# A routed kernel: five visits get the split second product, and the third token tile another PSUM bank

## The chip, the cores and the metric

The kernel runs on one core of a Trainium2 chip. A time is device microseconds (us) of one execution. Beside the plain runs there is one execution that was recorded instruction by instruction; all rows below come from it. PE is TensorE, PEld its weight loads, DVE is VectorE, ACT is ScalarE, POOL is GpSimd and SP is SyncE, which here only issues transfers. A small q (SPq, POOLq) is the sequencer of an engine. [...]

## The reference, cut to what matters

Two stages. The first is a convolution over time with seven taps whose weights come from a softmax per position and head; the second is a mixture of experts with two levels of choice, 4 groups of 4 experts, one expert per token.

```
w = softmax(weight_gen, axis=-1)                      # 8 x 2880 positions, 8 heads, 7 taps
x = sum_k w[:, s, h, k] * x_pad[:, s + k, h, :]       # 23040 tokens of 192
g = argmax(x @ w_group);  e = argmax(x @ w_expert[g])
out = softmax(..)[g] * softmax(..)[e] * (relu(x @ w1[g, e]) @ w2[g, e])   # w1 192x1024, w2 1024x192
```

## The kernel before

**Front and visits.** The tokens are cut into fifteen groups of 1536. For each group the front makes the softmax, the convolution in two chunks of six columns (`conv`; a chunk is seven products and six additions on DVE, 128x1152 each), the scores (`logits`: six pieces, each of three transposes on PE and a copy by ACT, then 48 small matmuls and a last transpose), the ranking (`ranks`, on DVE) and twelve scatters of token rows by POOL (`scatter_row`) into a table sorted by expert. Behind some groups a table of visits is made (`table`, `listing`). A visit takes 128, 256 or 384 rows of one expert, loads its rows and weights through SP (`load`: part 0 rows `xb`, parts 1 and 2 the first weights, part 3 the second), transposes the rows on PE (`prep_x`), and does the two products (`gemm1`, `gemm2`). What comes out is scaled and written to its places by POOL (`send`, L962). `ROUNDS` says how many visits of which size stand behind which group. The last four rounds are: behind the twelfth group one visit of 384 and four of 256; behind the thirteenth (index 11 of `ROUNDS`) five of 256; behind the fourteenth (index 12) six of 256; behind the fifteenth and last (index 13) ten of 384, six of 256 and two of 128. Behind the fifteenth group POOL also writes sixteen blocks of padding rows (L559).

**Order of the work.** PE, ACT, DVE and SP run in the order in which the program emits their instructions. The emission is interleaved by a planner with clocks of its own (`clk`). A visit is a row of units: four of two slices of the inner width for 256 rows, eight of one slice for 384. In a unit the planner emits `gemm1` of the unit, then preparations for the next visit (at unit 0 `block(nxt)` and the copy `prep_d`, at unit 1 `prep_x(nxt, 0)`, and for a visit of 384 its third tile, `prep_x(nxt, 2)`, at unit `last // 2 + 1`, which is 2 while a visit of 256 runs and 4 while one of 384 does), then `gemm2` of the unit two before (`LAG`), then at most one weight split, then what waits in the queues `late`, `held` and `later` (DVE work, by `flush`), and at last `fill`, which takes steps of the front until DVE's planned clock is ahead of PE's by `AHEAD`.

**A step of the front.** `step()` resumes the front's generator until it next yields a cost. Beside the convolution, `routing` moves the scores by one piece per unit and only when the ranking of the group ahead is done. Behind the last group's convolution nothing is left but `settle`, which moves with a limit of 99; in `move` that limit lifts the one piece per unit:

```
if what == "time" and v > clk["dve"] or what == "unit" and v == state["unit"] and most < HURRY or ...:
    return
```

So the step that ends the last chunk of the last group (it sets `o.chunks` to 2) goes on and emits every remaining piece of `logits`, the 48 matmuls and the last transpose before it comes to the first cost, that of `ranks`.

**Whole and split second product.** `whole(n)` is true for visits of 128 and, below the round `WHOLE`, for the others. A whole visit keeps hidden values and second weights as float32 and does one matmul of 192 columns per slice and token tile (L945). A split visit rounds the hidden values (`hh`, L918), makes their remainder on DVE (`hl`, DVE at L840 into `pr`), casts the second weights on ACT (L832) and makes their remainder on DVE, in two halves of a visit (`split`, part 3), and does a matmul of 384 columns (L947) and one of 192 (L948) per slice and tile. The remainder's scaled add is one more DVE instruction per tile (L960). The weights of a split visit arrive in one buffer (`raw[2]`), so the next visit's part 3 is asked for when the second half is split. `hl` takes the three `pr` buffers of the convolution, so no convolution may come after the first split visit; `block` sees to that by taking all steps of the front.

**Banks.** `tpx` (pool `ps_x`, one bank) takes the transposed rows of two tiles, or of the third tile. ACT copies them out rounded (`xh`, L887) and DVE makes the remainder (`xl`, L840) from the same bank; until then the bank is not free. `tp` (pool `ps_t`, one bank) is used by the visits of 128, at L870 to L874, and by every other piece of `logits` (L387 to L399). The rows `xb` of a visit of 256 lie in a buffer that was that of the visit six before, and its part 0 waits until POOL's writes of that visit have landed, as they read their places from it.

Of the kernel before, what the change touches and what calls it, by code (L numbers as in the profile page):

```python
# [9 lines left out]
F32 = mybir.dt.float32  # L10
# [9 lines left out]
WIDTHS = (12,) * 15  # L20
# [3 lines left out]
HURRY = 12  # L24
SPACED = range(2, 15)
HALVES = (36.0, 42.0, 48.0, 54.0, 60.0, 66.0, 72.0, 78.0)
WHOLE = 12
SINGLE = tuple((k,) for k in range(7))
MIXED = ((0, 1), (2,), (3,), (4,), (5,), (6,))
TURNED = ((6, 5), (4,), (3,), (2,), (1,), (0,))  # L30
# [11 lines left out]
def conv_moe_kernel(ctx: ExitStack, tc: tile.TileContext, x, wgen, w_group, w_expert, w1, w2, out):  # L42
# [5 lines left out]
    P = 128  # L48
# [7 lines left out]
    SC = 6  # L56
# [13 lines left out]
    ENDS = [r[0] for r in ROUNDS]  # L70
# [27 lines left out]
    ps_x = pool("ps_x", 1, space=PSUM)  # L98
    ps_t = pool("ps_t", 1, space=PSUM)
# [12 lines left out]
    grp = {}  # L112
# [129 lines left out]
    def run(eng, cost, *deps):  # L242
        clk[eng] = max([clk[eng]] + [d + HOP for d in deps]) + cost
        return clk[eng]
# [484 lines left out]
    def step():  # L729
        c = next(fr, None)  # L730
        if c is None:
            return False
        if isinstance(c, Until):
            clk["dve"] = max(clk["dve"], c)
        elif c is not NEXT:
            run("dve", c + 0.06)
        if state["starve"] or not state["slots"] and c is NEXT:
            state["unit"] += 1
        return c
# [18 lines left out]
    def plain(n):  # L758
        return order[n][1] == 1
# [107 lines left out]
    def prep_x(b, t0):  # L867
        fill(b.o.tx)
        if b.plain:
            tp = ps_t.tile([P, 3, P], F32, name="tp")  # L870
# [5 lines left out]
            b.txl = 0.0  # L876
            return
        m = min(2, b.nt - t0)
        tp = ps_x.tile([P, 2, 2, P], F32, name="tpx")[:, :, 0:m]
        for t in range(m):  # L880
            nc.tensor.transpose(out=tp[:, 0, t, :], in_=b.x[:, t0 + t, 0:P], identity=ident)  # L881
            nc.tensor.transpose(out=tp[:, 1, t, :], in_=b.xd[:, t0 + t].rearrange("p a b -> p (a b)"), identity=ident)  # L882
# [94 lines left out]
    def whole(n):  # L977
        r, nb, q = order[n]
        return nb == 1 or n < nmain and r < WHOLE

# [8 lines left out]
    def blocks(n0, n1, paced):  # L989
# [44 lines left out]
        def block(i):  # L1034
            n = units[i][0]
            o = visits[n]
            b = Slot()
            b.th = {}
            b.plain, b.nt = plain(n), order[n][1]
            b.wide = b.nt == 3  # L1040
            b.nv = 1 if b.wide else 2
            b.n = b.nt * P
            b.o, b.h, b.x = o, {}, o.xb
            b.clears = n == nmain - 4
            if not b.plain:
                while state["open"]:
                    assert step() is not False
                state["slots"] = True
            if not o.whole:
                while step() is not False:  # L1050
                    pass
            return b

        lead = range(n0, min(n0 + 3, n1))
# [28 lines left out]
        for i in range(len(units) + LAG):  # L1083
# [25 lines left out]
            if i < len(units):  # L1109
# [7 lines left out]
                for job in list(jobs):  # L1117
                    m, part, h = job
# [60 lines left out]
```

## Time and profile before

| | |
|---|---|
| median of 3 runs | 1201.04 us (1196.92 to 1202.0) |
| the profiled execution | 1193.24 us, of it 1191.6 us span |
| mean granted clock of TensorE | 0.989 |
| busy share of the span | PE 95%, PEld 90%, DVE 81%, ACT 55%, POOL 48% |

Busy time of a matmul overlaps with the next one's, since matmuls are pipelined; so steps on PE are measured from start to start here, and not by adding durations. Times in the rows are from the span's start.

### The profile page before, as it was taken

What the parts mean: (1) busy time and instruction counts of PE and PEld (TensorE: products, weight loads), DVE (VectorE), ACT (ScalarE), POOL (GpSimd) and SP (SyncE); (2) the same over time, 40 slices, a digit from 0 to 9 for tenths busy, and PEclk for the clock granted to TensorE, in tenths of its full rate; (3) what the DMA queues carried; (4) which work ended last, traced back from release to release, by engine and by line L of the source; (5) the groups of instructions that cost most, each with busy time, mean ns of one, the idle gap of its engine ahead of it and who ended that gap; (6) DMA issues with size and microseconds to landing.
All of it is one profiled execution on the core that took longest, in us unless ns stands there. A gap on an engine that the chain in (4) does not pass through costs nothing.

```text
span 1191.6 us, 24474 instructions
## 1 busy us (share of the span) xinstructions
PE 1132.8 (95%) x8357; PEld 1073.7 (90%) x8357; DVE 959.7 (81%) x1646; ACT 651.2 (55%) x1235; POOL 569.1 (48%) x608
## 2 busy tenths in 40 slices
PE   5787899999999999999999999999999989999998
PEld 3444788999999999999999999999899989999997
DVE  8899898999998999899999999898535756666661
ACT  1331345565565655655655655655556766666572
POOL 6154183756273747575656555374664112222211
PEclk9997999999999999999999999999999999999999
DMA  5698799887888877888687878558688675555562
GB/s 172 212 308 224 264 303 308 267 266 249 255 253 261 282 221 239 274 253 264 211 298 228 281 223 293 186 160 257 203 271 256 217 196 159 160 161 159 164 200 76
DMA packets 82758, 275.08 MB, mean 231 GB/s; under 512 B 15063, under 2 KB 31734, under 8 KB 80832
## 3 DMA queue, kind: packets, MB, share of 16 engines
q1 hardware_dynamic: 62296, 229.76, 61.9%
q0 software_dynamic: 20208, 43.39, 11.5%
q8 instruction: 67, 1.10, 0.4%
q14 instruction: 67, 0.55, 0.2%
q10 hardware_dynamic: 120, 0.28, 0.1%
HBM read 225.83 MB, written 48.42 MB: 230 GB/s over the span
## 4 chain that ended last, share of the span: by engine, by line
PE 58%; issue 20%; DVE 7%; DMA 6%; POOL 5%; SPq 2%; ACT 1%; POOLq 1%; DVEq 0%; ACTq 0%
PE py L945 26%; PE ph L907 24%; POOL out L962 4%; DVE pr L294 3%; PE pl L375 2%; DMA raw<-w1lo 1%; PE tpx L882 1%; DMA out<-y,xb 1%; PE tpx L881 1%; DMA wt<-in_weight_gen 1%; DMA w1lo<-raw 1%; DMA xb<-rows 1%; PE ph L335 1%; PE tp L392 1%; POOLq L557 1%
## 5 line engine op out<-in xcount | busy, mean ns | idle before, releaser
L907 PE MATMUL ph<-xh,wa 128*128 128x256 f32 (+1 forms) x1992 | 465.5, 307 | 0.0
L962 POOL DMA_INDIRECT out<-y,xb x189 | 204.9, 1084 | 438.7 <-DVE y L960 193.8
L945 PE MATMUL py<-wc,hh 128*128 128x192 f32 x2160 | 399.9, 326 | 2.1 <-ACT y L954 2.1
L907 PE MATMUL ph<-xl,wa 128*128 128x256 f32 (+1 forms) x1328 | 360.2, 290 | 0.3 <-DVE xl L840 0.3
L945 PEld LDWEIGHTS py<-wc,hh 128*128 128x128 f32 x2160 | 346.4, 190 | 2.4 <-ACT y L954 2.3
L907 PEld LDWEIGHTS ph<-xh,wa 128*128 128x128 f32 x1992 | 337.5, 190 | 3.3 <-issue 1.8
L913 ACT ACTIVATE hh<-ph 128x512 f32<-128x512 f32 (+2 forms) x296 | 165.5, 559 | 262.0 <-PE ph L907 261.8
L294 DVE TENSOR_TENSOR pr<-xin,wt 128x1152 f32<-128x1152 f32 x186 | 248.9, 1350 | 5.5 <-PE py L335 3.5
L907 PEld LDWEIGHTS ph<-xl,wa 128*128 128x128 f32 x1328 | 251.9, 190 | 0.6 <-DVE xl L840 0.6
L503 POOL DMA_INDIRECT rows<-xrow,ix x156 | 227.4, 1457 | 49.4 <-POOL ix L502 35.8
L312 DVE TENSOR_TENSOR xrow<-xrow,pr 128x1152 f32<-128x1152 f32 x144 | 194.6, 1351 | 0.7
L840 DVE SCALAR_TENSOR_TENSOR pr<-ph,hh 128x384 fp32r<-128x384 f32 (+1 forms) x128 | 77.5, 606 | 99.8 <-ACT hh L918 98.6
L840 DVE TENSOR_TENSOR wa<-raw,wa 128x1024 fp32r<-128x1024 f32 x83 | 101.4, 1222 | 31.1 <-ACT wa L816 30.9
L947 PE MATMUL py<-wc,hh 128*128 128x384 f32 x352 | 110.6, 362 | 0.0
L918 ACT ACTIVATE hh<-ph 128x384 fp32r<-128x384 f32 (+1 forms) x128 | 68.4, 534 | 69.8 <-PE ph L907 69.8
L502 POOL COPY ix<-posi 128x1 int32<-128x1 int32 x156 | 70.0, 458 | 63.7 <-DMA rows<-xrow,ix 36.2
L816 ACT CAST wa<-raw 128x1024 fp32r<-128x1024 f32 x83 | 87.2, 1050 | 3.1 <-DMA raw<-in_moe_w 3.1
L948 PE MATMUL py<-wc,pr 128*128 128x192 f32 x352 | 88.0, 250 | 0.0
L825 ACT CAST wa<-raw 128x1024 fp32r<-128x1024 f32 x83 | 86.7, 1045 | 0.6 <-DMA raw<-w1lo 0.6
L954 ACT ACTIVATE y<-py,xb 128x192 f32<-128x192 f32 x179 | 67.1, 422 | 21.4 <-PE py L945 19.7
L840 DVE TENSOR_TENSOR xl<-tpx,xh 128x512 fp32r<-128x512 f32 (+1 forms) x94 | 61.5, 655 | 17.0 <-ACT xh L887 16.2
L948 PEld LDWEIGHTS py<-wc,pr 128*128 128x128 f32 x352 | 67.1, 191 | 0.0
(178 smaller groups left out, 1341.8 us busy)
## 6 DMA issues: line engine op xcount, KB each, us to landing
wc<-in_moe_w SPq DMA_DIRECT2D x73, 768.0 KB, 5.8
raw<-in_moe_w SPq DMA_DIRECT2D x83, 512.0 KB, 5.4
xin<-in_x SPq DMA_DIRECT2D x14, 1728.0 KB, 10.0
raw<-in_moe_w SPq DMA_DIRECT2D x91, 256.0 KB, 5.2
raw<-w1lo SPq DMA_DIRECT2D x83, 256.0 KB, 5.4
raw<-in_moe_w SPq DMA_DIRECT2D x22, 768.0 KB, 6.8
xb<-rows SPq DMA_DIRECT2D x72, 194.0 KB, 3.8
wa<-in_moe_w SPq DMA_DIRECT2D x24, 384.0 KB, 5.0
```

The lines of the kernel that those rows point to most:

```text
L294: nc.vector.tensor_tensor(out=dst, in0=o.xin[:, c0 + k:c0 + k + SC, :].rearrange("p s (h g) -> p s h g", g=HG), in1=w4[:, c0:c0 + SC, :, k ...
L312: nc.vector.tensor_tensor(out=acc, in0=acc, in1=prs[k - 2], op=ALU.add)
L503: written_once(nc.gpsimd.indirect_dma_start(out=rows[:, :], out_offset=bass.IndirectOffsetOnAxis(ap=ix, axis=0), in_=src, in_offset=None, ...
L816: nc.scalar.copy(out=o.wa[:, 0, :], in_=o.raw[0])
L825: nc.scalar.copy(out=o.wa[:, 2, :], in_=o.raw[1])
L840: f(*a, **k)
L907: nc.tensor.matmul(ph[:, v, :], lhsT=w[:, f0:f0 + P], rhs=rhs, start=i == 0, stop=i == len(terms) - 1)
L913: nc.scalar.activation(out=hh, in_=ph, func=AF.Relu)
L945: nc.tensor.matmul(b.acc[t], lhsT=hh[:, v, c], rhs=wc[0][:, f, :], start=f == 0 and not (b.wide and t == 1), stop=f == NFT - 1 and not (b. ...
L947: nc.tensor.matmul(b.py[t], lhsT=hh[:, v, c], rhs=wc[f // 4][:, f % 4].rearrange("p l d -> p (l d)"), start=f == 0, stop=False)
L948: nc.tensor.matmul(b.acc[t], lhsT=hl[:, v, c], rhs=wc[f // 4][:, f % 4, 0, :], start=False, stop=f == NFT - 1)
L962: ins = nc.gpsimd.indirect_dma_start(out=out[:, :], out_offset=bass.IndirectOffsetOnAxis(ap=b.x.bitcast(I32)[:, t, D + 1:D + 2], axis=0), ...
```

## The change

Three edits. `WHOLE` goes from 12 to 11, so the five visits of 256 behind the thirteenth group become split ones. The third tile of a visit of 384 (`t0` is 2) is transposed into `tp` instead of `tpx`; that concerns the ten visits behind the fifteenth group and the one behind the twelfth. And `block` no longer takes all steps of the front before a split visit, but steps until the last group's convolution is done. The first split visit is now the first one behind the thirteenth group, so that loop runs one round earlier, at unit 0 of the last visit behind the twelfth group.

```
-WHOLE = 12
+WHOLE = 11
...
-        tp = ps_x.tile([P, 2, 2, P], F32, name="tpx")[:, :, 0:m]
+        tp = ps_t.tile([P, 2, 1, P], F32, name="tp") if t0 else ps_x.tile([P, 2, 2, P], F32, name="tpx")[:, :, 0:m]
...
             if not o.whole:
-                while step() is not False:
-                    pass
+                while grp[ENDS[-1] - 1].chunks * SC < WIDTHS[-1]:
+                    assert step() is not False
             return b
```

## Rows read from the trace of the kernel before

**Rows 1.** The page, part 1: busy us, share of the span, instructions.

```profile
PE 1132.8 (95%) x8357; PEld 1073.7 (90%) x8357; DVE 959.7 (81%) x1646; ACT 651.2 (55%) x1235; POOL 569.1 (48%) x608
```

**Rows 2.** Timeline of PE, first transpose for a visit: start, us, engine, line.

```profile
879.65 0.27 PE L881 MATMUL tpx<-ident,xb 128*128 128x128 f32 x1
890.06 0.27 PE L881 MATMUL tpx<-ident,xb 128*128 128x128 f32 x1
...
910.61 0.33 PE L881 MATMUL tpx<-ident,xb 128*128 128x128 f32 x1
...
920.90 0.27 PE L881 MATMUL tpx<-ident,xb 128*128 128x128 f32 x1
...
932.29 0.27 PE L881 MATMUL tpx<-ident,xb 128*128 128x128 f32 x1
...
942.05 0.27 PE L881 MATMUL tpx<-ident,xb 128*128 128x128 f32 x1
```

**Rows 3.** Timeline of DVE: end of the last convolution, end of the ranking.

```profile
828.96 1.35 DVE L294 TENSOR_TENSOR pr<-xin,wt 128x1152 f32<-128x1152 f32 x1
...
832.80 2.74 DVE L312 TENSOR_TENSOR xrow<-xrow,pr 128x1152 f32<-128x1152 f32 x2
...
857.77 0.17 DVE L489 SCALAR_TENSOR_TENSOR posi<-pos 128x12 int32<-128x12 f32 x1
```

**Rows 4.** Timeline of PE around the last group's scores.

```profile
828.34 1.47 PE L945 MATMUL py<-wc,hh 128*128 128x192 f32 x8
...
832.56 0.38 PE L392 MATMUL tp<-ident,xrow 128*128 128x128 f32 x2
...
838.22 0.38 PE L392 MATMUL tp<-ident,xrow 128*128 128x128 f32 x2
...
844.23 0.48 PE L907 MATMUL ph<-xh,wa 128*128 128x256 f32 x2
```

**Rows 5.** Timeline of ACT: second chunk's `rem`, first wide visit's second weights.

```profile
839.12 0.52 ACT L385 COPY rem<-xrow 128x384 f32<-128x384 f32 x1
...
959.68 0.84 ACT L832 CAST wc<-raw 128x768 fp32r<-128x768 f32 x1 [0.68 <-DMA raw<-in_moe_w]
```

**Rows 6.** Windows: stretch, its us, busy us (x) of PE, PEld, DVE, ACT, POOL; clock; DMA.

```profile
955.00:960.00 5.00, 1.82 (x14) 1.85 (x15) 2.42 (x3) 1.27 (x4) 1.51 (x2) 1.00 0.69 202
...
120.00:130.00 10.00, 7.72 (x87) 6.55 (x86) 6.56 (x7) 4.74 (x11) 0.00 (x0) 0.83 0.89 343
```

**Rows 7.** Third tile: three PE timeline stretches, then PEld's waits (total, times, longest).

```profile
958.18 0.30 PE L881 MATMUL tpx<-ident,xb 128*128 128x128 f32 x1 [3.44 <-DVE xl L840]
...
971.16 0.34 PE L907 MATMUL ph<-xl,wa 128*128 128x384 f32 x1
971.34 0.27 PE L881 MATMUL tpx<-ident,xb 128*128 128x128 f32 x1
...
985.80 0.34 PE L907 MATMUL ph<-xl,wa 128*128 128x384 f32 x1
986.13 0.33 PE L881 MATMUL tpx<-ident,xb 128*128 128x128 f32 x1
...
PEld tpx L881 <- DVE xl L840: 2.5, 8, 0.3
```

**Rows 8.** Groups by line and form, DVE, 760 to 920 us: busy us, mean ns.

```profile
L840 DVE SCALAR_TENSOR_TENSOR pr<-ph,hh 128x512 fp32r<-128x512 f32 x7 | 4.8, 691 | 10.1 <-ACT hh L918 10.1
L840 DVE TENSOR_TENSOR wc<-raw,wc 128x768 fp32r<-128x768 f32 x4 | 3.8, 951 | 2.5 <-ACT wc L832 2.5
```

**Rows 9.** Timelines of POOL (last padding block) and of SP (rows' load).

```profile
901.18 0.67 POOL L559 DMA_DIRECT2D rows<-rem  x1 [0.78 <-issue]
...
907.92 0.33 SPq L779 DMA_DIRECT2D xb<-rows  x1
```

**Rows 10.** Timelines of PE and DVE around the earlier visit of 384's third tile.

```profile
773.52 0.38 PE L392 MATMUL tp<-ident,xrow 128*128 128x128 f32 x2
...
773.58 0.42 DVE L840 TENSOR_TENSOR xl<-tpx,xh 128x256 fp32r<-128x256 f32 x1 [1.18 <-ACT xh L887]
```

## The prediction

> **What bounds the kernel now.** I read the page first: PE is busy 95% of the span and its weight loads 90%, DVE 81%, the rest far less [rows 1]. So a change has to shorten PE's row of instructions or its holes, and the other engines matter where PE stands still for them. Then PE's timeline over the last rounds. One landmark returns in every visit, the first transpose for the next visit at unit 1, and from one to the next is a visit's length: 10.41 us for a whole visit of 256 behind the thirteenth group (879.65 to 890.06), 9.76 us for a split one that nothing disturbs (932.29 to 942.05) [rows 2]. Third, what makes PE stand still there: the wide visits' third tile [rows 7], the scores of the last group [rows 4], and two visits of the next round whose rows and weights come late [rows 2, 9].
>
> **Part 1, five visits get the split second product.** Five visits times 10.41 less 9.76 is 3.25: I take -3.2 us. That holds if DVE, ACT and the weight loads keep up. What a split visit adds on DVE is four remainders of 0.69 us and two of the weights of 0.95 us, 4.7 us in a visit of 9.8 [rows 8], and two scaled adds. The cover is the time in which the convolution is over: it ends at 832.80 + 2.74 = 835.5 [rows 3], before these visits start at 844.23 [rows 4]. Not free is the stretch in which the last group is ranked (until 857.9, [rows 3]) and its table made; the planner then puts front steps and remainders in turn. Weights that land late are the other danger: in the round behind, one split visit took 920.90 to 932.29, 11.39 us instead of 9.76, so 1.63 us lost [rows 2]. For the five visits I bound such stalls by 0 below and by two of that size, 3.3, above, and take +1.0, since with a landing in time the neighbours lose nothing.
>
> **Part 2, the loop in `block`.** The loop runs where the last visit behind the twelfth group has just emitted the first product of its unit 0; on PE that product ends at 828.34, where a second product starts [rows 4]. DVE is then in the last group's last chunk: the product at 828.96 and the two additions at 832.80 are still to come [rows 3]. The trouble is what the last forced step does. It is the step that sets `o.chunks` to 2, and that step runs on through `settle`, whose limit of 99 lifts the one piece per unit. So all six pieces of the scores, the 48 matmuls and the last transpose are emitted there, in front of three units of ready work. Before, that burst came after the convolution's end in time: 838.22, with two of the pieces spread out earlier (one at 832.56) [rows 4]. Now PE reaches it at 828.34 and its second chunk has to wait for DVE. DVE does what is left without the weight and `xl` remainders in between, so the convolution ends at 828.96 + 1.35 + 2.74 = 833.0. From the copy `rem` of the second chunk to the next first product it was 839.12 to 844.23, 5.1 us [rows 4, 5], so PE gets free at about 838.1: 9.8 us after 828.34. The scores cost PE 844.23 - 838.22 = 6.0 and about 0.5 for the two spread pieces before. The difference is +3.3 us; I take +3.2. Below I bound it by 2.0 (some pieces of the first chunk overlap better), above by the same and a fall of the clock, next.
>
> In the hole PE does nothing for some 2 to 3 us. A hole of 3.44 us [rows 7] left the granted clock at 1.00, the upper level, in the window around it [rows 6]. [...] The upper bound of part 2 is thus 3.2 + 1.7 = 4.9.
>
> What follows the burst gets its scores 6 us earlier, but the five visits now share DVE with the ranking; I expect the ranking's end near where it was, 857.9 [rows 3], and the table and the padding later, because DVE has only some 3 us per visit for them.
>
> **Part 3, the third tile's bank.** In nine wide visits behind the first the old bank costs little: PEld waits for `xl` 8 times, 2.5 us in all, 0.3 each. On PE the step from the last matmul of the unit to the transpose is 0.33 us (985.80 to 986.13) where it waits and 0.18 (971.16 to 971.34) where it doesn't, and the transpose itself is longer (0.33 for 0.27) [rows 7]; that is 0.2 us each. I take 8 x 0.2 = -1.6, between 0 and -2.5.
>
> For the first wide visit PE stands 3.44 us [rows 7], because the third tile follows the first two by only one unit while a visit of 256 runs. The other bank removes this wait. What is late next? ACT's next work behind the third tile's copy is the cast of the second weights at 959.68, which waited 0.68 us for the transfer itself [rows 5]; the relu of the last unit stands behind it in ACT's queue, its remainder behind that on DVE, and the third tile's `xl` after it. If the weights land when they did, all this moves up by at most 0.68 us, and PE, which needs that `xl` for the wide visit's first product, stands there instead. So -0.6, with 0 as one end and the whole 3.4 as the other.
>
> At the earlier wide visit the new bank costs something: the third tile's `xl` reads the bank until 773.58 + 0.42 = 774.0, and a piece of the scores writes `tp` from 773.52 [rows 10]. That piece now waits: +0.5 (0 to 0.5). At the tail, the visits of 128 use `tp` long after the last wide one; nothing there.
>
> **Part 4, the round behind the fourteenth group.** Two steps there are longer than 9.76: 910.61 to 920.90 by 0.53 and 920.90 to 932.29 by 1.63 [rows 2]. Their rows' load, at 907.92, waited for writes of an earlier visit that stood in POOL's queue behind the last of sixteen padding blocks (901.18) [rows 9], and the weight loads stood behind it in SP's queue. If the table comes later, those writes get ahead of the padding and the load is early. I take -1.6 of the 2.2, between 0 and -2.2.
>
> **The sum.** -3.2 + 1.0 + 3.2 - 1.6 - 0.6 + 0.5 - 1.6 = -2.3 us: 1193.24 becomes 1190.9. The profiled execution was faster than the median of the runs, 1201.04; in its proportion the forecast for the median is 1198.7. All low ends together give -3.2 + 0 + 2.0 - 2.5 - 3.4 + 0 - 2.2 = -9.3, or 1191.7 for the median; all high ends -3.2 + 3.3 + 4.9 + 0 + 0 + 0.5 + 0 = +5.5, or 1206.6.
>
> **Rivals.**
> 1. *Faster: the first wide visit's stall goes whole.* If the second weights land about 3 us sooner than at 959.6, the cast is no longer what is late, and the third tile saves 3.4 instead of 0.6. With no stalls of the five visits' own and the burst at its low end it is -2.3 - 2.8 - 1.0 - 1.2 = -7.3, so 1193.7 on the median's scale. For it: the wait for the transfer was short, and SP is less blocked if part 4 holds. Against it: the load can't be asked for before the buffer is free.
> 2. *Slower: the fifteenth group's ranking ends late and POOL's chain with it.* If the split work of two visits (2 x 4.7 us) goes ahead of the ranking on DVE and the early scores bring nothing, the ranking ends at 867.2 instead of 857.9, the scatters and padding follow 9.4 us later, and rows that were there for the transpose at 910.61 come at 920.0. PE would be ready at 910.6 - 3.2 + 3.2 + 0.5 + 1.0 = 912.1 and waits 7.9 us; part 4's relief is gone too: -2.3 + 1.6 + 7.9 = +7.2, or 1208.3. It decides from a ranking that ends some 8 us late on. For it: the load at 907.92 was just in time before. Against it: the scores come 6 us sooner, and the planner gives DVE's free time to the front before the table.
> [...]
> 4. *The five visits gain nothing,* since PE waits in each for a remainder or a late weight: that is the upper end of part 1, +3.3 instead of +1.0, so 0.0 in all, 1201.0.
>
> **Chances and range.** The forecast has 0.45, the third rival 0.05, the fourth 0.10; all three lie within 0.5% (6.0 us), which is about what a measurement of this kernel can tell from no change. The first rival has 0.27, the second 0.13. So faster by over 0.5% has 0.27, within it 0.60, slower 0.13. The range for 8 in 10 takes in the bounds' sum on the fast side and stops short of the second rival: 1192 to 1206. The forecast's own range is 1195 to 1202.
>
> **What would show it.** Right: from landmark to landmark 9.8 us in the five visits; six pieces of the scores and the 48 matmuls in one stretch right behind a first product near 828, with PE idle for 2 to 3 us before the second chunk, the wait named `rem` from DVE's convolution; no wait of the third tile for `xl`, and in its place, before the first wide visit's first product, a wait of up to 3 us for the third tile's `xl` behind the cast of the second weights; the padding blocks later than 901 and the rows' load no longer behind them. Wrong: no hole near 831, so the burst lies elsewhere; a first wide visit that starts without a wait, so the weights came earlier; steps over 11 us in the five visits, with remainders on DVE or the weights' transfer as the releaser; or a wait for rows of 5 us and more in the next round, which is the second rival.

## The result and the profile after

The changed kernel takes 1207.48 us (median of 13 runs, 1203.68 to 1212.29), the kernel before on the same chip 1198.28 (13 runs): a ratio of 1.0071, 95% interval 1.0052 to 1.0089. The change makes the kernel slower by 0.7%. The profiled execution of the changed kernel took 1203.68 us, its span 1201.8, its mean granted clock 0.983 (a share: 1.00 in a row is full speed).

The page's first part, as [rows 1] for before: us busy, share, instructions.

```profile
PE 1135.7 (95%) x8357; PEld 1078.5 (90%) x8357; DVE 983.6 (82%) x1686; ACT 658.8 (55%) x1245; POOL 571.6 (48%) x608
```

DVE and ACT have the 24 us and 8 us of remainders and casts that five more split visits bring. PE is busy longer, though the split visits ask less of it: it ran more of its work at a lower granted clock (0.983 in the mean, 0.989 before).

The first transposes of each visit, the landmark of [rows 2], tell where the time went. The table gives how much longer a stage became, once by the two profiles already named and once by two more, of both kernels on one chip (runs e5_before and e6_after below).

| stage | forecast | changed less before | e6_after less e5_before |
|---|---|---|---|
| up to the visits behind the twelfth group (same program) | 0 | +4.0 | -2.8 |
| wide visit behind the twelfth group | +0.5 | +0.6 | +0.6 |
| burst of scores, with the visit that holds it | +3.2 | +5.4 | +5.4 |
| the five split visits | -2.2 | -1.0 | -0.4 |
| round behind the fourteenth group | -1.6 | +2.3 | +4.1 |
| first wide visit behind the fifteenth group | -0.6 | +1.0 | -3.5 |
| eight later wide visits | -1.6 | -1.8 | -1.5 |
| rest | 0 | -0.1 | -0.1 |
| sum from the second row on | -2.3 | +6.3 | +4.6 |

The first row is chance: the programs are the same there, and the sign differs between the pairs. The sums run to PE's last products. The medians differ by more, 9.2 us here and 6.4 on the chip of the second pair; what the rest is, no profile shows.

**The burst.** PE's timeline there, which answers to [rows 4] (start, us, engine, line, operation, idle before and its releaser), then DVE's end of the convolution and of the ranking, which answers to [rows 3]:

```profile
833.08 0.38 PE L392 MATMUL tp<-ident,xrow 128*128 128x128 f32 x2
...
837.94 0.66 PE L392 MATMUL pl<-ident,xrow 128*128 128x128 f32 x2 [2.10 <-DVE xrow L430]
...
840.96 2.79 PE L375 MATMUL pl<-xT,wr 128*32 128x128 f32 x48 [0.57 <-ACT xT L399]
844.40 0.59 PE L419 MATMUL pl<-ident,xT 128*128 128x128 f32 x3 [0.65 <-ACT xT L411]
844.83 1.47 PE L945 MATMUL py<-wc,hh 128*128 128x192 f32 x8
```

```profile
835.05 2.75 DVE L312 TENSOR_TENSOR xrow<-xrow,pr 128x1152 f32<-128x1152 f32 x2
...
868.03 0.17 DVE L489 SCALAR_TENSOR_TENSOR posi<-pos 128x12 int32<-128x12 f32 x1
```

All pieces stand in one stretch from 833.08; the convolution ends 4.7 us later, as worked out, and PE is back at its visits after 11.75 us, not 9.8. The 48 matmuls take 2.79 us, against 1.52 where the clock is 1.00 (below). Stretches of this trace (us; busy us and count of PE, PEld, DVE, ACT, POOL; granted clock; DMA share; GB/s):

```profile
837.00:839.00 2.00, 1.06 (x5) 0.85 (x6) 0.95 (x3) 0.55 (x2) 1.84 (x2) 0.68 0.03 9
839.00:841.00 2.00, 1.43 (x10) 0.70 (x10) 0.00 (x0) 1.40 (x3) 1.57 (x2) 0.50 0.28 97
841.00:843.00 2.00, 2.00 (x40) 1.85 (x44) 0.00 (x0) 0.00 (x0) 1.54 (x3) 0.50 0.17 60
843.00:845.00 2.00, 1.35 (x21) 0.88 (x14) 0.00 (x0) 0.48 (x1) 1.71 (x3) 0.62 0.29 103
```

The granted clock is 0.50 from the end of the hole (837.94) to the burst's last transposes (844.40), and 1.00 from 845 on. From the earlier wide visit on (its third tile, 772.00 in before, 776.02 after) the ranking ends at 85.8 us in before [rows 3] and at 92.0 after: 6 us later, though its scores were emitted earlier.

**The round behind the fourteenth group.** ACT, PE, POOL and SP there, which answer to [rows 9]:

```profile
919.35 0.83 ACT L832 CAST wc<-raw 128x768 fp32r<-128x768 f32 x1 [6.11 <-DMA raw<-in_moe_w]
```

```profile
922.24 0.33 PE L881 MATMUL tpx<-ident,xb 128*128 128x128 f32 x1 [2.72 <-DMA xb<-rows]
```

```profile
907.81 1.31 POOL L962 DMA_INDIRECT out<-y,xb  x1 [0.30 <-issue]
...
914.78 0.68 POOL L559 DMA_DIRECT2D rows<-rem  x1 [0.62 <-issue]
```

```profile
914.57 0.33 SPq L779 DMA_DIRECT2D xb<-rows  x1
```

The same write of results in before:

```profile
903.51 1.01 POOL L962 DMA_INDIRECT out<-y,xb  x1 [0.30 <-issue]
```

The last pad is issued at 914.78 where it was at 901.18. The load of these rows waits until the results of the second visit behind the thirteenth group are written, whose rows lay in the same buffer. The second of these two writes stood behind all pads (903.51); now it stands ahead of six of the sixteen (907.81). In the stretch from the earlier wide visit's third tile on it is no later: 131.5 us behind it in before, 131.8 now. But the load is issued 6.8 us behind that write, where it was 4.4, and the rows are transposed 7.7 us behind the load, where it was 2.7 (907.92 to 910.61). PE waits 2.72 us for them. In e6_after the two steps are 9.3 and 7.8 us, in e5_before 3.5 and 2.3. The DMA engines are fuller at that place. Stretches of before, then of the changed kernel:

```profile
900.00:910.00 10.00, 10.00 (x79) 10.00 (x78) 6.22 (x9) 5.98 (x11) 7.11 (x8) 1.00 0.68 197
910.00:920.00 10.00, 9.80 (x74) 9.37 (x73) 4.28 (x7) 4.83 (x9) 4.17 (x4) 1.00 0.98 302
```

```profile
900.00:910.00 10.00, 9.39 (x74) 9.16 (x73) 8.63 (x25) 6.59 (x12) 6.92 (x10) 1.00 0.99 269
910.00:920.00 10.00, 9.52 (x74) 9.31 (x72) 3.86 (x6) 3.69 (x7) 6.66 (x9) 1.00 1.07 304
```

**The first wide visit**, which answers to [rows 7]: PE, ACT and two stretches.

```profile
966.06 0.27 PE L881 MATMUL tp<-ident,xb 128*128 128x128 f32 x1
...
973.46 0.44 PE L907 MATMUL ph<-xl,wa 128*128 128x384 f32 x1 [3.21 <-DVE xl L840]
```

```profile
971.02 0.83 ACT L832 CAST wc<-raw 128x768 fp32r<-128x768 f32 x1 [3.48 <-DMA raw<-in_moe_w]
```

```profile
973.00:975.00 2.00, 1.54 (x8) 1.55 (x9) 1.46 (x4) 0.79 (x3) 0.00 (x0) 0.81 0.81 202
975.00:977.00 2.00, 2.00 (x8) 2.00 (x8) 1.23 (x2) 1.11 (x2) 0.00 (x0) 0.50 1.04 336
```

The third tile no longer waits; the wait is where the prediction put it, before the first product that reads the third tile's `xl`, behind the cast of the second weights.

### The profile page after: what moved, and what is told of

Read it like the earlier page. It is cut to its first block, busy times and chain, and to the rows that moved or that the text cites. A ratio compares the mean times of both kernels' runs of the same rounds, so it can differ in the third digit from the quotient of the medians.

```text
span 1201.8 us, 24517 instructions
## 1 busy us (share of the span) xinstructions
PE 1135.7 (95%) x8357; PEld 1078.5 (90%) x8357; DVE 983.6 (82%) x1686; ACT 658.8 (55%) x1245; POOL 571.6 (48%) x608
## 4 chain that ended last, share of the span: by engine, by line
PE 60%; issue 16%; DVE 9%; DMA 8%; POOL 3%; ACT 2%; SPq 1%; POOLq 0%; ACTq 0%; DVEq 0%
PE ph L907 26%; PE py L945 25%; DVE pr L294 3%; POOL out L962 3%; DMA raw<-in_moe_w 2%; PE pl L375 2%; PE py L947 1%; DMA raw<-w1lo 1%; PE tpx L882 1%; PE tpx L881 1%; DMA wa<-in_moe_w 1%; DVE xrow L312 1%; DMA w1lo<-raw 1%; DMA xb<-rows 1%; PE tp L392 1%
## 5 line engine op out<-in xcount | busy, mean ns | idle before, releaser
L962 POOL DMA_INDIRECT out<-y,xb x189 | 205.9, 1089 | 445.4 <-DVE y L960 193.4
L945 PE MATMUL py<-wc,hh 128*128 128x192 f32 x2000 | 371.8, 327 | 2.2 <-ACT y L954 2.2
L945 PEld LDWEIGHTS py<-wc,hh 128*128 128x128 f32 x2000 | 322.0, 191 | 2.4 <-ACT y L954 2.4
L913 ACT ACTIVATE hh<-ph 128x512 f32<-128x512 f32 (+2 forms) x276 | 153.6, 557 | 245.6 <-PE ph L907 245.0
L840 DVE SCALAR_TENSOR_TENSOR pr<-ph,hh 128x384 fp32r<-128x384 f32 (+1 forms) x148 | 91.3, 617 | 103.9 <-ACT hh L918 103.7
L947 PE MATMUL py<-wc,hh 128*128 128x384 f32 x432 | 136.5, 365 | 1.7 <-DVE y L960 1.7
L918 ACT ACTIVATE hh<-ph 128x384 fp32r<-128x384 f32 (+1 forms) x148 | 80.4, 543 | 78.1 <-PE ph L907 77.8
L948 PE MATMUL py<-wc,pr 128*128 128x192 f32 x432 | 108.9, 252 | 0.0
L947 PEld LDWEIGHTS py<-wc,hh 128*128 128x128 f32 x432 | 82.2, 190 | 2.7 <-DVE y L960 2.1
L948 PEld LDWEIGHTS py<-wc,pr 128*128 128x128 f32 x432 | 83.3, 193 | 0.0
```

The lines of the kernel that those rows point to most:

```text
L840: f(*a, **k)
L913: nc.scalar.activation(out=hh, in_=ph, func=AF.Relu)
L945: nc.tensor.matmul(b.acc[t], lhsT=hh[:, v, c], rhs=wc[0][:, f, :], start=f == 0 and not (b.wide and t == 1), stop=f == NFT - 1 and not (b. ...
L947: nc.tensor.matmul(b.py[t], lhsT=hh[:, v, c], rhs=wc[f // 4][:, f % 4].rearrange("p l d -> p (l d)"), start=f == 0, stop=False)
L948: nc.tensor.matmul(b.acc[t], lhsT=hl[:, v, c], rhs=wc[f // 4][:, f % 4, 0, :], start=False, stop=f == NFT - 1)
L962: ins = nc.gpsimd.indirect_dma_start(out=out[:, :], out_offset=bass.IndirectOffsetOnAxis(ap=b.x.bitcast(I32)[:, t, D + 1:D + 2], axis=0), ...
```

## The experiments

The runs fell on several chips of two kinds. On one kind the kernel before takes 1198 to 1200 us, on the other 1233 to 1235; each ratio is against runs of the kernel before on the same chip. M is the stretch in the profile from the third tile of the earlier wide visit (772.00 in before) to the first transposes of the first wide visit behind the fifteenth group (951.80): 179.8 us in before, 187.2 in the changed kernel.

| run | edit | before, us | ratio, 95% interval | M, us |
|---|---|---|---|---|
| e1_bank | bank alone | 1232.85 | 0.9988 [0.9961, 1.0015] | 183.4 |
| e2_loop | early loop alone | 1232.85 | 1.0091 [1.0056, 1.0125] | 194.4 |
| e3_marker | changed, scores ten us later | 1232.85 | 1.0038 [1.0018, 1.0057] | 191.8 |
| e4_paced | changed, scores piece by piece | 1232.85 | 1.0046 [1.0020, 1.0072] | 192.8 |
| e5_before | before, again | 1199.81 | one run, 1200.2 us | 180.8 |
| e6_after | changed, again | 1199.81 | 1.0046 [1.0010, 1.0081] | 190.2 |
| e7_fill | changed, hole filled | 1199.81 | 1.0026 [1.0003, 1.0048] | 187.4 |
| e8_three | bank, three split visits | 1199.81 | 1.0003 [0.9977, 1.0029] | 183.2 |
| e9_pads | before, pads on SP | 1233.29 | 0.9966 [0.9937, 0.9994] | 183.3 |
| e10_three_pads | e8 and pads on SP | 1233.29 | 0.9979 [0.9948, 1.0009] | 183.2 |
| e11_after_pads | changed, pads on SP by four | 1233.29 | 1.0122 [1.0073, 1.0170] | 199.2 |
| e12_after_pads_fill | e11 and e7 | 1233.29 | 1.0142 [1.0094, 1.0190] | 210.7 |
| e13_after_pads2 | changed, pads on SP by two | 1198.78 | 1.0074 [1.0051, 1.0096] | 193.4 |
| e14_bank_pads | bank, pads on SP | 1198.78 | 0.9970 [0.9945, 0.9995] | 178.2 |
| e15_three_pads | e14 and three split visits | 1198.78 | 1.0002 [0.9980, 1.0024] | 181.8 |
| e16_after_raw2 | changed, second raw buffer | 1235.36 | 1.0062 [1.0022, 1.0101] | 200.9 |
| e17_three_pads_raw2 | e15 and second raw buffer | 1235.36 | 0.9954 [0.9918, 0.9989] | 184.2 |
| e18_bank_pads_raw2 | e14 and second raw buffer | 1235.36 | 0.9942 [0.9909, 0.9976] | 181.8 |

The kernels whose loop stays late have an M of 178.2 to 184.2 on either kind of chip; all with the early loop have 187.2 or more.

**The edits apart.** e1_bank is before with the bank's line alone; e2_loop is before with the loop also at the visits behind the thirteenth group, which stay whole:

```
-            if not o.whole:
-                while step() is not False:
-                    pass
+            if not o.whole or order[n][0] == 11:
+                while (grp[ENDS[-1] - 1].chunks * SC < WIDTHS[-1] if order[n][0] == 11 else step() is not False):
+                    assert order[n][0] > 11 or step() is not False
```

> Only the third tile's other bank; every visit and the loop stay as before. Theory A (the bank is a small gain, and the loss of the whole change lies elsewhere): the eight later wide visits gain 1.8 us together, the earlier wide visit loses 0.5, the first wide visit gains 0.6, so about 1196.4 us, a ratio of 0.998. Theory B (the wait that the bank moves from the transposes to the subtraction's result lets the clock fall behind it, as in the changed kernel's trace): the first wide visit loses 1.0 in place of gaining 0.6, the sum is about 0, a ratio of 1.000. Theory C (the bank itself costs the change's 0.7%): 1206 us. The profile tells A from B: granted clock in the 6 us behind the hole of the first wide visit, 1.00 by A, near 0.5 in one stretch of 2 us by B.

> Only the forced loop one round earlier: the five visits behind the thirteenth group keep the whole second product, the third tile keeps its bank. Theory A (the early burst of scores is the largest loss): the stretch between the first transposes of the visits around it grows by 5.4 us as in the changed kernel, with a stretch of granted clock near 0.5; the ranking then ends no later than before, so the round behind the fourteenth group keeps its time: about 1203 us, a ratio of 1.004. Theory B (the loss comes from the split visits' load on VectorE): no more than 1 us at the burst and a ratio within 0.001 of 1.

The bank alone is not to be told from no change (0.9988), so theory C falls. Its ratio lies between those of theories A and B; in its profile theory B came true, with a wait of 3.28 us for the third tile's `xl` and the clock at 0.50 behind it. The loop alone, with not one split visit, gives 1.0091. Of the 11.0 us by which its M is longer than that of e1_bank, 9.8 stand in the two visits around the burst (38.2 us for 28.4); the round behind the fourteenth group takes 52.1 us for 51.5. The changed kernel itself was not timed on this chip. The burst of e2_loop:

```profile
868.08 0.66 PE L392 MATMUL pl<-ident,xrow 128*128 128x128 f32 x2 [2.04 <-DVE xrow L430]
...
871.11 2.79 PE L375 MATMUL pl<-xT,wr 128*32 128x128 f32 x48 [0.57 <-ACT xT L399]
878.34 0.90 PE L419 MATMUL pl<-ident,xT 128*128 128x128 f32 x3 [4.45 <-issue]
```

It is the same hole and the same fallen clock (2.79 us again), and another 4.45 us ahead of the scores' last transposes, which the changed kernel's own trace has as 0.65 and e1_bank as 1.18. Without the 3.3 us by which this wait is longer than that of e1_bank, the 9.8 would be 6.5, an estimate, against 5.4 in the table. Such waits stand at the bursts of other early-loop traces of this kind of chip too (3.80 us in e11_after_pads, 8.03 in e16_after_raw2). ACT's copy ahead of these transposes waits too, 6.76 us in e2_loop, and the profile names no engine of this core that released it; what it waits for stayed open.

**The scores later.** e3_marker and e4_paced add a stop to the changed kernel behind the last convolution, and e4_paced lets `settle` keep to one piece per unit:

```
-            yield from finish_all(side)
+            yield from finish_all(side if g < ENDS[-1] - 1 else [(yield NEXT)][1:])
...
-                yield from move(qs, q, 99)
+                yield from move(qs, q, 99 if g < ENDS[-1] - 1 else HURRY - 1)
```

> The whole change, with a mark behind the last group's convolution at which the loop stops, so that the scores stand four steps (some 10 us) later in TensorE's queue. Theory A (most of the loss is TensorE waiting at the burst for the convolution, and the clock that falls in that wait): the burst shrinks from 11.75 us to 5 to 5.5, granted clock 1.00 in it, the ranking ends some 3 us later than in the changed kernel and costs about 1 more in the round behind the fourteenth group: about 1202 us, a ratio of 1.003. Theory B (the loss is the late POOL chain): 1209 us or more, a ratio of 1.009, since the ranking is later still.

> As the one with the mark, and the scores' pieces are put between the steps of the visits one by one in place of in one burst. Theory A: nearly the whole hole goes, 6 to 8 us at the burst against the changed kernel, and the ranking ends 5 us or more later than in it, which gives some of it back in the round behind the fourteenth group: about 1202 us (1198 to 1205), a ratio of 1.003. Theory B (the POOL chain decides): a ranking 5 us later costs 5 us in that round: 1206 us or more, a ratio of 1.006.

Both come 0.45 to 0.53% below the loop alone on the same chip, and their ratios are near those of theory A. That does not show theory A, since e2_loop lacks the bank and the split visits, and M is 191.8 and 192.8 for 194.4 there. In e3_marker the burst still takes 10.1 us and not 5 to 5.5: the clock is 1.00 in its 48 matmuls, but a wait of 3.43 us like the one above follows, with the clock at 0.50 behind it. Its ranking ends 122.9 us behind the earlier wide visit's third tile, where the changed kernel has 92.0, and its round behind the fourteenth group takes 59.1 us. In e4_paced the hole is gone, the pieces stand in visits of ordinary length; but the ranking now ends 143.4 us behind the earlier wide visit's third tile, in place of 92.0, and the hole is back at the first wide visit:

```profile
999.25 0.47 PE L881 MATMUL tpx<-ident,xb 128*128 128x128 f32 x1 [18.90 <-DMA xb<-rows]
```

So a ranking that is late enough does hold PE, by rows, as rival 2 said. The changed kernel's ranking is only 6 us late.

**The clock, and three visits without the early loop.** e7_fill gives the changed kernel 26 transposes of the identity in the hole; e8_three keeps the first two of the five visits whole and the drain of before at the round behind:

```
-            for u in range(2):
-                nc.tensor.transpose(out=tp[:, u, :], in_=row[:, u, 0:P], identity=ident)
+            for u in ((2, 2) * 9 if s2 == SC else ()) * (g == ENDS[-1] - 1) + (0, 1) + ((2, 2) * 4 if s2 == 0 else ()) * (g == ENDS[-1] - 1):
+                nc.tensor.transpose(out=tp[:, u, :], in_=row[:, u, 0:P] if u < 2 else ident, identity=ident)
```

```
-        return nb == 1 or n < nmain and r < WHOLE
+        return nb == 1 or n < nmain and (r < WHOLE or r == WHOLE and q < 2)
```

> The kernel before, unchanged, once more with a profile, for its steps from visit to visit beside those of the other runs of this group. Expected by every theory: from the first transposes of the second visit behind the twelfth group on, the same steps as in the profile shown of before, within 0.5 us each, while the stretch up to 770 us may differ by 4 us or more from run to run; if a chip adds waits of its own, they stand at the same places here and in the other runs.

> The changed kernel, unchanged, once more: 0.5 to 0.9% slower than before by every theory. Its profile tells whether the granted clock falls again behind the two holes (the burst of scores, the first wide visit): by theory A (the fall follows from the hole's length and place) in both again, to about 0.5 for 4 us or more at the burst; by theory B (chance) in neither or in one.

> The changed kernel with 26 transposes of the identity put where TensorE waits in the burst of scores (8 while the first remainder is copied, 18 while VectorE ends the convolution); they stand in tiles that the real transposes then overwrite. Theory A (the clock falls because TensorE idles there, and the fall costs 1.9 us): granted clock 1.00 through the burst, the stretch from the copy of the second remainder to the next visit's work 5.1 us in place of 6.95, so 1.5 to 2 us (0.15%) faster than the changed kernel. Theory B (the fall comes from the kind of work, small matmuls and transposes, whether or not TensorE waits): the clock falls all the same and the time is that of the changed kernel or up to 1 us longer.

> The bank edit, and the split second product in the last three of the five visits behind the thirteenth group only, so that the loop stands where the convolution has been given out anyway; the drain at the first visit behind the fourteenth group as before. Theory A (the early loop is what costs, the split itself gains): 0.65 us gained by each of three visits and 0 to 2 us by the bank, no early burst: 1 to 3 us faster than before, a ratio of 0.998. Theory B (splits next to the ranking cost more than they save): a ratio of 1.001 to 1.004, with waits for raw weights and VectorE in those three visits.

e7_fill, PE and stretches of its trace:

```profile
834.30 2.18 PE L392 MATMUL pl<-ident 128*128 128x128 f32 x18
...
839.03 1.52 PE L375 MATMUL pl<-xT,wr 128*32 128x128 f32 x48 [0.57 <-ACT xT L399]
```

```profile
837.00:839.00 2.00, 1.21 (x7) 0.73 (x7) 0.00 (x0) 1.34 (x3) 1.41 (x4) 1.00 0.14 50
839.00:841.00 2.00, 1.52 (x48) 1.25 (x48) 0.00 (x0) 0.33 (x1) 1.84 (x3) 1.00 0.30 104
```

The clock stays at 1.00, the 48 matmuls are back at 1.52 us, and the visit with the burst takes 20.28 us in place of 22.04 in e6_after: 1.8 us, theory A. In e6_after the clock fell at the burst (0.50) and not at the first wide visit (1.00), where its hole was 1.99 us and not 3.21.

At the first wide visit e5_before has before's own hole once more, 3.45 us [rows 7], and this time the clock fell behind it:

```profile
964.11 0.30 PE L881 MATMUL tpx<-ident,xb 128*128 128x128 f32 x1 [3.45 <-DVE xl L840]
```

```profile
964.00:966.00 2.00, 1.89 (x9) 1.92 (x10) 0.00 (x0) 0.99 (x2) 0.00 (x0) 0.63 0.19 67
966.00:968.00 2.00, 2.00 (x10) 2.00 (x10) 0.00 (x0) 0.22 (x1) 0.00 (x0) 0.51 0.53 148
```

One program, one place, one length, and the clock at 1.00 in one execution ([rows 6], and in every 2 us from there to 968) and at 0.51 in the next: the visit took 1.6 us longer. In e9_pads it fell behind one of 3.51 us, to 0.50. The fall in one of the two places of e6_after is what its theory B said, though its second hole was shorter; these pairs show the same for one length: of two holes of 3.44 and 3.45 us, the clock fell behind one.

e8_three is no faster than before, near theory B. Beside e5_before, the five visits with its three split ones save 1.5 us, and then the round behind the fourteenth group is 3.4 us longer (55.7 us for 52.2). PE's wait for rows there and the issue of their load, in e5_before and then in e8_three:

```profile
916.85 0.33 PE L881 MATMUL tpx<-ident,xb 128*128 128x128 f32 x1 [1.29 <-DMA xb<-rows]
```

```profile
914.53 0.33 SPq L779 DMA_DIRECT2D xb<-rows  x1
```

```profile
916.80 0.33 PE L881 MATMUL tpx<-ident,xb 128*128 128x128 f32 x1 [2.91 <-DMA xb<-rows]
```

```profile
906.75 0.33 SPq L779 DMA_DIRECT2D xb<-rows  x1
```

The rows come at the same time in both, but not because something fixes that time. e8_three asks for them 7.8 us earlier, and they take 10.1 us where e5_before has 2.3. From 900 to 910 us the DMA engines' share is 1.05 in e8_three and 0.74 in e5_before; POOL issues ten pads from 895 to 920 us in each, and what SP's transfers move there grows from 2.88 to 4.10 MB. What PE gained was waited away, and the fallen clock behind that wait took more (0.94 from 910 to 920 us and 0.89 from 920 to 930, where e5_before has 1.00).

e8_three has no early loop, and its ranking ends 86.4 us behind the earlier wide visit's third tile (85.9 in e5_before); e2_loop has the early loop, and its round is 0.6 us longer than that of e1_bank. So the loss in this round comes with split visits, and neither the early loop nor a late ranking is needed for it.

**The pads off POOL.** The rows' load waits for writes of results, which stood behind the pads. The next runs issue the pads from SP, so many at a time, with the front's stop between:

```
             for e in range(NE):
+                if e and e % 2 == 0:
+                    yield Until(clk["pe"] + 2.0)
-                rv = nc.gpsimd.value_load(pfi[0:1, e:e + 1], min_val=0, max_val=NROW - BK)
+                rv = nc.sync.value_load(pfi[0:1, e:e + 1], min_val=0, max_val=NROW - BK)
...
-                ins = nc.gpsimd.dma_start(out=rows[bass.ds(rv, BK), :].rearrange("(p t) c -> p t c", t=2), in_=pad2)
+                ins = nc.sync.dma_start(out=rows[bass.ds(rv, BK), :].rearrange("(p t) c -> p t c", t=2), in_=pad2)
...
-                if e % 4 == 3:
-                    yield NEXT
```

> The kernel before with the last round's sixteen padding writes issued by SP, two at a time between its loads, in place of by POOL one behind the other (the drain at the first visit behind the fourteenth group becomes the changed kernel's loop). Theory A (what holds the rows of the round behind the fourteenth group is POOL: the writes of the results, which free the row tiles, stand behind the pads): the wait of 1.3 us for rows and the clock loss behind it go, some 2 to 3 us: a ratio of 0.998. Theory B (the loads are late because the DMA queues are full, not because of POOL's order): no gain, a ratio of 1.000 to 1.003, since the pads then crowd the weights on SP's queue.

> The same on top of the bank edit and the three late split visits. Theory A (the gain of the split visits was swallowed by the rows that came at the time POOL set, whatever TensorE did): now 2 us of the splits, 1 to 2 of the bank and 2 to 3 of the pads show together: 4 to 6 us faster than before, a ratio of 0.996. Theory B (the splits cost as much as they save, by VectorE and the weights): the ratio is that of the pads alone, within 0.001.

> The changed kernel with the padding writes issued by SP, four at a time. Theory A (rival 2 of the prediction, the POOL chain, took 3 to 4 us of the changed kernel's loss): the waits of 2.7 to 4.2 us for rows and of 6.1 for weights in the round behind the fourteenth group go, 3 us or more faster than the changed kernel: a ratio of 1.003. Theory B (POOL's chain is only a symptom, VectorE with the ranking and the tables next to five split visits is the bound): less than 1 us, a ratio of 1.005 or more.

> The run before this with the 26 transposes of the identity in the burst's hole. If the two costs are separate they add: 1.8 us faster than that run and a ratio of about 1.001, so that what remains of the changed kernel's loss is the wait for the convolution of some 3.5 us less the gains of the bank and the splits; if the time that the clock gives back is swallowed by a later wait, the ratio is that of the run before this.

Before gains by it (e9_pads 0.9966; the run has the changed kernel's loop in place of the drain too, which was not tried alone). With the bank and three split visits on top it is 0.9979, not told from that. The changed kernel does not: by fours, eight pads stood ahead of one rows' load on SP, which was issued at 955.60, and PE waited 4.42 us; a miss of this experiment's own, and e12's added fill can't be read on top of it. The next group repeats it by twos:

> The changed kernel with the padding writes issued by SP, two at a time (with four at a time, eight of them stood ahead of one load of rows, which was issued at 955.6 us and made TensorE wait 4.4 us). Theory A (the POOL chain took 3 to 4 us of the changed kernel's loss in the round behind the fourteenth group): no wait for rows above 1 us there, and a ratio against the kernel before that is 0.003 below the changed kernel's, 1.002 to 1.004. Theory B (any order of these writes costs as much, since the ranking ends late): waits for rows or weights of 3 us or more in that round, a ratio of 1.005 or more.

> The kernel before with the bank edit and the padding writes on SP two at a time; no split visit. Expected: the 0.34% of the pads and 0.1% of the bank add to a ratio of 0.9955. If the bank's gain is only the later start of a wait for weights, it is that of the pads alone, 0.9966.

> The same with the split second product in the last three of the five visits, beside the run without it. Theory A (a split visit gains 0.5 to 0.65 us wherever rows do not hold TensorE): 1.5 to 2 us faster than the run without, a ratio of 0.994. Theory B (the split visits' work on VectorE delays the ranking and the tables and gives it back): the same time as the run without, or slower.

e13_after_pads2 is at 1.0074, theory B: without POOL's pads in the way PE still waits for rows, now three visits later. The load, issued at 948.43, stands on SP behind two pads (942.72) and a wait of 3.8 us for the one raw buffer, so the pads are not wholly out of its way.

```profile
954.68 0.47 PE L881 MATMUL tpx<-ident,xb 128*128 128x128 f32 x1 [3.32 <-DMA xb<-rows]
```

e14_bank_pads is faster than both kernels, 0.9970, and in its trace PE has no wait for rows or weights in the two rounds. e15_three_pads differs from it by three split visits alone and is 0.3% slower by the medians, little beside the noise. Stretches of the two, e14_bank_pads first:

```profile
860.00:880.00 20.00, 20.00 (x148) 19.97 (x147) 14.06 (x70) 10.96 (x20) 14.65 (x20) 1.00 0.85 258
880.00:925.00 45.00, 45.00 (x337) 44.80 (x336) 18.61 (x25) 28.86 (x50) 15.91 (x19) 1.00 0.92 268
```

```profile
860.00:880.00 20.00, 20.00 (x149) 19.81 (x147) 16.86 (x75) 13.07 (x22) 14.41 (x21) 1.00 0.61 187
880.00:925.00 45.00, 42.38 (x321) 41.35 (x321) 28.32 (x42) 27.10 (x47) 16.08 (x18) 1.00 1.00 282
```

With the split visits the DMA engines do less up to 880 (share 0.61 against 0.85), then are full (1.00), and PE is idle for 2.6 us. The same shift stands in e8_three beside e5_before (0.54 for 0.77, then 0.92 for 0.78) and in the changed kernel beside before (0.74 for 0.85, then 0.95 for 0.78). The code has a possible reason: a whole visit's second weights go straight into one of four buffers (`wc`), a split visit's pass the one raw buffer. SP's waits in the changed kernel and in e5_before, 840 to 960 us (us in total, times, longest):

```profile
SPq L803 <- DVE wc L840: 31.9, 10, 5.8
```

```profile
SPq L803 <- DVE wc L840: 15.5, 4, 5.8
```

SP's queue stands behind each: in the changed kernel it was held 31.9 us in ten waits, and it issues nothing between 851.35 and the load at 857.79, which waited 5.8 us. Between e15 and e14 themselves these waits are 15.6 us for 11.0, and those for the first weights' buffer (`wa`) 24.4 for 27.6, so that the raw buffer makes the shift is argued and not shown.

**A second raw buffer.**

```
-                o.raw = [f(i) for f in new_raw]
+                o.raw = [f(i) for f in new_raw[0:2]] + [new_raw[2](i) if i % 2 or r < WHOLE or whole(n) else state["raw2"] ...]
```

where `raw2` is a tile of the convolution's input pool.

> The changed kernel with a second buffer for the raw second weights of the split visits (a tile that the convolution no longer needs), used by every other split visit. Theory A (a split visit's second weights pass one raw buffer, SP holds its whole queue until VectorE has done the subtraction that reads it, and rows and weights behind it come late): SP's waits for that subtraction between 840 and 960 us fall from 32 us to 10 or less, the split visits' and the next round's waits shrink by 2 to 4 us: a ratio of 1.004 against the kernel before. Theory B (the rows of results, or the ranking, hold that round whatever the weights do): the SP wait goes and the time stays, a ratio of 1.006 to 1.008.

> Bank edit, three late split visits, padding writes on SP, and the second raw buffer. Theory A: without SP's hold the three split visits keep their 0.5 us each: 1 us or more faster than the run with the second buffer and without split visits, and 4 us or more faster than the same kernel with one raw buffer: a ratio of 0.996 or less. Theory B: the ratio stays at 1.000.

> Bank edit, padding writes on SP, second raw buffer, no added split visit: the control for the run before this. Expected by both theories: 0.997 as without the second buffer, or up to 0.002 better if the raw loads of the visits behind the fourteenth and fifteenth groups come earlier too.

The waits on SP for that buffer are gone in all three; those for `wa` are longer instead (35.0 us in e17 where e10 has 26.6, from 865 to 985 us). The changed kernel still waits for rows:

```profile
963.76 0.48 PE L881 MATMUL tpx<-ident,xb 128*128 128x128 f32 x1 [5.33 <-DMA xb<-rows]
```

so for it theory B holds. Their load is issued 8.8 us behind the write that it waits for, and they come 8.8 us behind the load, as in the changed kernel without the second buffer. Between e17 and e18 the ratios put three split visits at a cost of 0.12%, where it was 0.32% between e15 and e14; but the medians of e17 and e18, 1230.26 and 1230.60, differ the other way, so neither a cost nor a part of the buffer in it is shown there. No run shows a gain from split visits.

## Why the prediction was wrong

The forecast was 1198.7 us, no change; measured 1207.48. On the profiles' scale the sum was -2.3 us and became +6.3 and +4.6. By its steps:

- **Part 2, the burst: right in place and mechanism, too small by 2.2 us.** The pieces, the wait for the second chunk and the convolution's end stand where they were put. The step that failed is "A hole of 3.44 us [rows 7] left the granted clock at 1.00", which took one execution's hole for a rule and left the fall to the upper bound and to a chance of 0.05; behind the same hole in e5_before, 3.45 us, the clock was at 0.51. It fell in the burst of all six profiles of the early loop with the hole in it; filling the hole gave 1.8 us back (20.28 for 22.04). No run shows the 1.7 us in this part's upper bound of 4.9; the 1.8 is what the runs have in its place. Of the 5.4 us that leaves 3.6, near the 3.2 taken.
- **Part 4, the relief: wrong sign, by 3.9 to 5.7 us.** The step that failed is "those writes get ahead of the padding and the load is early". The pads came later, and the writes got ahead of six of them, but the load was not early: the write took 6.8 and 9.3 us to let it go in place of 4.4 and 3.5, and the rows 7.7 and 7.8 in place of 2.7 and 2.3, with the DMA engines' share at 0.99 and 1.07 in the changed kernel. -1.6 became +2.3 and +4.1. This is rival 2's place, at a third to a half of its 7.9 us, but its mechanism, a late ranking, is not needed for it (e8_three). In e8_three it is SP's transfers that fill the engines (4.10 MB for 2.88, share 1.05 for 0.74); how much of it the later pads are in the changed kernel stays open.
- **Part 1, the split visits: -1.0 and -0.4 in place of -2.2.** Own stalls were taken as +1.0; they are 2.2 and 2.8, inside the bound of 3.3. The step that failed is "since with a landing in time the neighbours lose nothing": with the split visits the DMA share was 0.74 for 0.85 up to 880 us and 0.95 for 0.78 behind it, and the next round's rows came 7.7 us behind their load in place of 2.7. Three visits alone gain 1.5 us and lose 3.4 there (e8).
- **Part 3, the bank: right, but for the size of the first wide visit.** Eight wide visits give 1.8 and 1.5 us (1.6 said), the earlier one costs 0.6 (0.5 said), the first one's wait moved to the third tile's `xl`. That visit's length, from its first transposes to the next third tile, changed by +1.0 and -3.5, where -0.6 was said and 0 to -3.4 allowed. The clock had a part: it fell behind the wait in e5_before (0.51) and in the changed kernel (0.50) and not in the other two (1.00): 19.54 and 21.12 us in before and e5_before, 20.51 and 17.66 in the changed kernel and e6_after. Alone it is 0.9988, not told from 1.
- **The chances.** The third rival, at 0.05, is the clock's fall in the burst's hole, and it came (0.50). A wait for rows as in rival 2 came beside it, for another reason. Each rival was priced as if it came alone; the two together were not priced.

Of the kernels timed, the bank with the pads on SP is faster than before, 0.9970, and with the second raw buffer on the other kind of chip, 0.9942; the pads on SP without the bank have 0.9966, which is not told from either.

## What to carry to other kernels

Before work is forced ahead of time, ask what the last forced step brings with it, and price the hole with a fall of the clock behind it as the likely case: in the burst here it fell in six profiles of six. A gain in one stage counts only if the next stage's loads still come in time: look at the share of the DMA engines there, and at what the edit moves into that stretch. An edit that changes the buffer through which a load passes can change when it is issued, and what stands behind it in that queue: SP waited 31.9 us for the raw buffer in the changed kernel and 15.5 in e5_before.

## What the runs showed of the hardware

- **TensorE's clock** behind one and the same hole of 3.44 and 3.45 us stayed at 1.00 in one execution of before and fell to 0.51 in another (e5_before). In the early loop's burst it fell in six profiles of six: the 48 matmuls took 2.75 to 2.79 us behind a wait of 2.04 to 2.11 us in the changed kernel, e2, e11, e13 and e16, and the clock was 0.50 in e6_after. It stayed at 1.00, with 1.52 us for them, in e7_fill, where the hole was filled with transposes. In the late loop's burst, with no wait above 0.92 us ahead of them, they took 1.52 us in before, e14, e15 and e17, 1.91 in e1_bank and 2.29 in e18.
- **A load behind full DMA engines.** The same load of rows (194 KB) let PE go on 2.3 us after its issue in e5_before, where the engines' share from 910 to 920 us is 0.68, and 10.1 us after it in e8_three, where it is 1.05 from 900 to 910 and 0.95 from 910 to 920.
- **The same kernel on several chips** took 1198 to 1200 and 1233 to 1235 us. In early-loop traces of the second kind, and in e3_marker, stand waits ahead of the scores' last transposes (4.45 us in e2, 3.80 in e11, 8.03 in e16, 3.43 in e3), where the changed kernel's trace on the first kind has 0.65 and e13's 0.67.
